# Moving the value products inside a round, and a first-group norm built from four columns

## The chip, the core and the metric

The kernel runs on one core of one Trainium2 chip. A core has a matrix engine (PE in the profile), a vector engine (DVE), a scalar engine for activations (ACT), a general engine (POOL) and a queue that issues transfers (SP). Each takes its own instructions strictly in the order of the program and waits on semaphores for the others. The metric is device microseconds (us) of one execution.

## The reference

Causal attention (4 batches, 12 heads, 448 positions, head size 64) is followed by an RMS norm and a gated feed-forward layer, all in float32:

```python
scores = where(mask, -1e9, q @ k.T / 8); attn = softmax(scores)
x = (attn @ v)                       # joined over heads: 1792 tokens x 768
rms = sqrt(mean(x * x, axis=-1) + 1e-6)
xn = x / rms * rms_g
g = xn @ w_gate
out = (g * sigmoid(g) * (xn @ w_val)) @ w_out
```

## The kernel before

The tokens are cut into three groups. The first is 512 tokens: the first 256 queries of two batches. It has 12 attention units (numbers 0 to 11 here; a unit is one pair of heads of one batch), and units 12 to 23 belong to the second group. The feed-forward products of one group are interleaved with the attention of the next. The order on every engine is written by hand: a list of steps is run one by one, each step is one tick, and `post(n, f)` runs `f` after n more ticks. The table `T` holds those delays, and `READY_X` holds the ticks from which each part of x may be used.

The first stage consists of rounds of six steps. Round p issues, in program order: the score products of unit p+3 (`scores`, L191), the products of the probabilities with v of unit p (`products`, L274) with the copy of their result into x (L289), the transposes of the first head of unit p+1 (L248, into bank t), two free steps, and the transposes of the second head of unit p+1 (L248, into bank x). Around this stand:

- the softmax on DVE: mask and minimum (L200), then the exponentials on ACT (L203) and the sum with a tiny bias (L226), then reciprocals on DVE (`rs`, L212), then scaling by them on POOL (L208, four instructions a unit);
- copies of the transposes out of PSUM into `pt`: the first head on ACT (L254), the second on DVE (L252); the products with v need both;
- the unpacking of weights (`w_c` L374 on ACT, `w` L375 on POOL, L377 and L379 on DVE) and their split into a high and a low part (`w_h` L389 on ACT, `w_l` L391 on DVE or L102 on POOL), and the same split of x (`xh` L325 on ACT, `xl` L326 on DVE);
- the early parts of the feed-forward product (`ffn_part`, L435 to L437, three matmuls each), which stand in the two free steps.

The norm: `square` squares each finished 128 x 512 part of x on POOL and adds it to `acc` on POOL. After the sixth part, `rms` multiplies `acc` by a matrix of ones (L333, result 128 x 512, the same in every row), ACT takes the root (L335), and DVE takes the reciprocal in four pieces (L338). The first use of it is `gr` (L449), on DVE, which empties the first accumulator of the feed-forward product; `t_sb` (a tanh on ACT, L450, then L451 on DVE) follows. Bank t has one buffer, so that a new user of it waits until the reader of the last one is done.

Of the kernel before, what the change touches and what calls it, by code (L numbers as in the profile page):

```python
# [10 lines left out]
F32 = mybir.dt.float32  # L11
# [3 lines left out]
ALU = mybir.AluOpType  # L15
AF = mybir.ActivationFunctionType
# [4 lines left out]
DM = H * D  # L21
DFF = 1536
P = 128
NP = H // 2
# [3 lines left out]
W = 512  # L28
# [10 lines left out]
        for g in range(NG) for c in range(NP)}  # L39
ENDS = [max(i for i, u in enumerate(UNITS) if u[0] == g) + 1 for g in range(NG)]  # L40
# [1 line left out]


T = dict(c0=0, c1=1, c2=4, c20=9, c3=5, c30=10, c5=7, c50=14, exp=1, exp0=3, gt=1, hh=1, hl=4, ws=5, ld2=7,
         ld=4, ld1=11, lv=5, norm0=7, norm1=2, r1=5, so=3, wl=2, wl0=8, xl=2, xl0=9)
LOAD = (4, 12, 24, 36, 48, 60, 74)
CONVERT = (20, 32, 44, 62, 76)
SPLIT = (33, 45, 57)

READY_W, READY_X = (45, 57, 68), (40, 52, 64, 76, 87)  # L50
WR = 4
WARM = [9, 0, 0, 2]
EXTRA = 4
# [8 lines left out]
def attention_ffn(ctx: ExitStack, tc: tile.TileContext, qk0, qk1, qk2, v, v2, w, g, out, out2):  # L62
# [7 lines left out]
    nc = tc.nc  # L70
# [3 lines left out]
    def pool(name, bufs, at=ctx, **kw):  # L74
        return at.enter_context(tc.tile_pool(name=name, bufs=bufs, **kw))
# [3 lines left out]
    ps = pool("ps", 1, space=PSUM)  # L79
    wr_p = pool("wr", WR, side="left")  # L80
    ws_p = pool("ws", 4, side="left")
    ht_p = pool("ht", 4, ffn, side="left")
    rm_p = pool("rm", 1, ffn, side="left")
# [7 lines left out]
    st_p = pool("st", 5, att, side="right")  # L91

    def bank(tag, bufs=1):


        return ps.tile([P, W], F32, tag=tag, name=tag + "_ps", bufs=bufs)
# [4 lines left out]
    def pool_op(out_, a, op, b):  # L101
        nc.gpsimd.tensor_tensor(out_, a, b, op=op)  # L102


    ident = const.tile([P, P], F32, name="ident")
# [12 lines left out]
    ones = const.tile([P, P], F32, name="ones")  # L118
    nc.vector.memset(ones, 1.0)
    eps = const.tile([P, 1], F32, name="eps")  # L120
# [9 lines left out]
    def post(delay, fn):  # L130
        if delay <= 0:
            fn()
        else:
            later.setdefault(now[0] + delay, []).append(fn)
# [7 lines left out]
    xr, xh, xl, acc, xq = {}, {}, {}, {}, {}  # L142
# [15 lines left out]
    def load_v(p):  # L158
        if p < len(UNITS):
            _, kind, _, _, row, _ = UNITS[p]  # L160
            raw_v[p] = raw.tile([P, 2, 4, 2, D], F32, tag="v", name="v_r", bufs=3)
            if kind == 2:
                nc.sync.dma_start(out=raw_v[p][: KB[2]], in_=v2[row])
            else:
                nc.sync.dma_start(out=raw_v[p][:, 0, : NKB[kind]], in_=v[row, :, : NKB[kind]])
# [67 lines left out]
    def steps_t(p):  # L233

        if not 0 <= p < len(UNITS):
            return []
        _, kind, _, _, _, _ = UNITS[p]
        pr = hs[p]
        kb = KB[kind]

        def some(e):
            pt = pr["pt", e] = pt_p.tile([P, W], F32, tag=f"pt{e}", name="pt")
            ps = bank("x" if e and p < ENDS[1] + 1 else "t")
            at = 0
            for j in range(NKB[kind]):
                for o, wd in blocks(kind):
                    if kb * j < wd:
                        nc.tensor.transpose(ps[:kb, at: at + P],  # L248
                                            pr["sp"][e][:, o + kb * j: o + kb * (j + 1)], ident)
                        at += P  # L250
            if kind or (e and p < ENDS[0]):
                nc.vector.tensor_copy(pt[:kb, :at], ps[:kb, :at])  # L252
            else:
                nc.scalar.copy(pt[:kb, :at], ps[:kb, :at])  # L254

        return [lambda e=e: some(e) for e in (0, 1)]

    def steps_a(p):


        if not 0 <= p < len(UNITS):
            return []
        g_, kind, c, k, _, base = UNITS[p]
        pr = hs[p]
        kb, nq = KB[kind], QUERIES[kind]

        def products():
            for h in range(1 + (kind == 2)):
                at = 0
                for j in range(NKB[kind]):  # L270
                    q0, n = ((0, 2 * P), (P, P))[j] if kind == 0 else (D * h, (P, D)[kind - 1])
                    a0 = at + (D * h if kind == 2 else 0)
                    for e in (0, 1):
                        nc.tensor.matmul(  # L274
                            av_ps[e * D: (e + 1) * D, p % 2, q0: q0 + n], raw_v[p][:kb, h, j, e, :],
                            pr["pt", e][:kb, a0: a0 + n], start=(j == 0), stop=(j == NKB[kind] - 1))
                    at += n if kind == 0 else P

        def copy():
            if g_ == 2 and base == 0:  # L280
                if c < 3:
                    xq[c] = w64_p.tile([P, 2, XT], F32, tag="w64", name="xq")
                xr[g_, c] = xq[c % 3][:, c // 3]
            elif base == 0:
                xr[g_, c] = xr_p.tile([P, W], F32, tag="xr", name="xr")
            x = xr[g_, c][:, base: base + nq]
            if p == LAST[g_, c]:
                post(2, lambda: square(g_, c))
            (nc.scalar.copy if g_ == 1 else nc.vector.tensor_copy)(x, av_ps[:, p % 2, :nq])  # L289

        return [products, copy]


    rinv, waiting, ff = {}, [], {}

    def square(b, c):

        halves = [(0, HX), (HX, XT)] if b == 2 else [(0, W)]
        for j, (lo, hi) in enumerate(halves):
            x = xr[b, c][:, lo: hi]  # L300
            sq = rm_p.tile([P, W], F32, tag="sq", name="sq") if c else \
                rm_p.tile([P, W], F32, tag="acc", name="acc", bufs=2)
            sq = sq[:, : hi - lo]
            if b:
                nc.scalar.activation(sq, x, AF.Square)
            else:
                pool_op(sq, x, ALU.mult, x)
            if c == 0:
                acc[b, j] = sq
            else:  # L310
                pool_op(acc[b, j], acc[b, j], ALU.add, sq)
        if b == 2:
            return
        if c == NP - 1:
            post(T["r1"], lambda: rms(b, acc[b, 0]))
        waiting.append((b, c))

    def split_x():
# [8 lines left out]
            out=l, in0=x, scalar=gc, in1=f32(h), op0=ALU.mult, op1=ALU.subtract))  # L327
        xh[b, c], xl[b, c] = h, l

    def rms(b, sq):  # L330

        ps = bank("t")
        nc.tensor.matmul(ps, ones, sq, start=True, stop=True)  # L333
        r = rinv[b] = rm_p.tile([P, W], F32, tag="rms", name="rms", bufs=2)
        nc.scalar.activation(r, ps, AF.Sqrt, bias=eps, scale=1.0 / DM)  # L335
        for i in range(W // P):
            sl = slice(i * P, (i + 1) * P)
            post(i if b else 0, lambda sl=sl: nc.vector.reciprocal(r[:, sl], r[:, sl]))  # L338


    w64 = w.bitcast(I32).rearrange("u p (c t) -> u p c t", t=2)
# [388 lines left out]
    def round_steps(p):  # L730

        noop = [lambda: None]
        (s_, ts) = (f or noop for f in (steps_s(p + DP), steps_t(p + 1)))
        as_ = steps_a(p)

        def products():
            for f in as_:
                f()


        def scores():
            if p + 2 > 0:
                post(T["lv"], lambda: load_v(p + 2))
            s_[0]()

        def both():
            scores()
            products()

        ts = (ts + noop)[:2]  # L750
        return [both] + ts if p > ENDS[0] else [scores, products, ts[0]] + 2 * noop + ts[1:]

    def round_of_two(p):

# [28 lines left out]
    with tc.manual_schedule():  # L783
# [9 lines left out]
        for p in range(-DP, ENDS[1]):  # L793
            steps += round_steps(p)
            if p + 1 in ENDS:
                ends.append(len(steps))
# [10 lines left out]
        def at_tick(n, fn):  # L807
            prep.setdefault(n, []).append(fn)
# [7 lines left out]
        n = 0  # L816
        for t_, s, c in early:
            n = max(n, t_)
            while n % 6 not in (3, 4) and n < 87:
                n += 1  # L820
            at_tick(n, lambda s=s, c=c: ffn_part(s, (c,)))
            n += 1
# [19 lines left out]
        for s in range(2 * NU):  # L842
# [9 lines left out]
            n = s + 6 - 2 * NU  # L852
# [5 lines left out]
            for k0 in (0, 2, 4):  # L858
# [3 lines left out]
                i = 3 * (s % NU) + k0 // 2 + 1  # L862
# [14 lines left out]
                n = 3 * (s - 2 * NU + 2) + k0 // 2  # L877
# [26 lines left out]
        for v in range(NF):  # L904
            if v % 3 == 1 and v < 9:
                wo_sums(v // 3)
            for i in range(7):
                ps_ = quad_product(v, i)
                quad_result(v, i, ps_)
                if v + 1 < NF:  # L910
                    n = (0, 1, None, 2, None, 3, None)[i]
# [7 lines left out]
                if v + 2 < NF:  # L919
                    n = (None, None, 0, 1, None, 2, 3)[i]  # L920
# [18 lines left out]
        for q in range(21):  # L939
            i, p = divmod(q, 3)  # L940
# [58 lines left out]
```

## Time and profile before

| | |
|---|---|
| median of 3 runs | 700.14 us (699.67 to 701.06) |
| profiled execution | 702.16 us |
| its span, first to last instruction | 700.4 us |
| PE, DVE, ACT, POOL busy in 20 to 40 us | 15.89, 18.39, 16.30, 19.87 of 20 |
| the same in 40 to 60 us | 16.83, 13.22, 14.30, 16.88 of 20 |
| the same in 60 to 80 us | 15.79, 14.43, 15.49, 12.21 of 20 |
| the same in 80 to 100 us | 17.93, 19.89, 16.47, 9.44 of 20 |
| the same in 100 to 120 us | 20.00, 19.07, 13.60, 12.28 of 20 |

How to read it: the span begins at 0, the first stage goes to about 74 us, and then the feed-forward part of the first group starts, with the second group's attention between. Matmuls overlap, so a busy share of PE says little by itself; the waits say more. The granted clock of PE is 0.99 on average; stretches below 1.0 stand in the table by stretches.

### The profile page before, as it was taken

Reading aid. Unit: us, or ns where it says so; the run is one execution under the profiler, and the core shown is the slowest. Engines: PE = TensorE matmul, PEld = TensorE weight load, DVE = VectorE, ACT = ScalarE, POOL = GpSimd, SP = SyncE. Lnnn points to the kernel's source line nnn. Section 1 sums busy time; section 2 is a strip of 40 time slices with the busy share of each in tenths; the row PEclk is TensorE's granted clock in tenths of the full one; section 3 lists DMA queues with packets and bytes.
Section 4 is the critical chain, followed back from the end, with each engine's and each line's share of the span. In section 5 each row is a group of like instructions: output and inputs, shape, how many; then the busy total and the mean of one; then the engine's idle time right before and its main releaser. Section 6 shows DMA issues by size and latency. Waiting matters only on the chain. (4 is left out here: it accounts for less than half of the span.)

```text
span 700.4 us, 11930 instructions
## 1 busy us (share of the span) xinstructions
PE 671.0 (96%) x4106; PEld 550.9 (79%) x4106; DVE 536.9 (77%) x1029; ACT 371.6 (53%) x832; POOL 361.9 (52%) x313
## 2 busy tenths in 40 slices
PE   9878889999999999999999999997999999999997
PEld 6445667777777768777777777886999999999987
DVE  4976899989997667777687877396386868679973
ACT  6967876777685435436445353451433342445540
POOL 4988445545548534665776565552363536302220
PEclk9999999999999999999999999998999999999999
DMA  8746486868778547576767655333567576562541
GB/s 267 259 146 205 146 281 222 281 232 277 233 280 302 193 117 263 164 258 194 251 190 237 212 155 177 118 120 109 162 204 250 177 246 223 168 165 86 171 119 67
DMA packets 71355, 138.80 MB, mean 198 GB/s; under 512 B 7744, under 2 KB 39232, under 8 KB 71296
## 3 DMA queue, kind: packets, MB, share of 16 engines
q1 hardware_dynamic: 71296, 138.05, 60.3%
q8 instruction: 32, 0.52, 0.3%
q14 instruction: 27, 0.22, 0.1%
HBM read 104.21 MB, written 33.82 MB: 197 GB/s over the span
## 5 line engine op out<-in xcount | busy, mean ns | idle before, releaser
L208 POOL TENSOR_SCALAR sp<-sp,rs 128x384 f32<-128x384 f32 (+3 forms) x132 | 89.5, 696 | 95.8 <-DVE rs L212 84.8
L435 PE MATMUL m_ps<-xh,w_h 128*128 128x512 f32 x282 | 120.2, 426 | 3.7 <-DVE rs L212 3.7
L203 ACT ACTIVATE sp<-sp,nm 128x384 f32<-128x384 f32 (+3 forms) x168 | 87.2, 522 | 47.7 <-DVE nm L200 47.1
L437 PE MATMUL m_ps<-xh,w_l 128*128 128x512 f32 x282 | 111.3, 395 | 0.0
L436 PE MATMUL m_ps<-xl,w_h 128*128 128x512 f32 x282 | 111.1, 394 | 0.0
L102 POOL TENSOR_TENSOR a_l<-w_q,a_h 128x768 fp32r<-128x768 f32 x24 | 47.4, 1977 | 75.7 <-ACT a_h L473 75.6
L375 POOL TENSOR_SCALAR w<-w 128x768 f32<-128x768 f32 x36 | 46.5, 1292 | 53.1 <-ACT w_c L374 47.0
L274 PEld LDWEIGHTS a_ps<-pt,v_r 128*64 128x64 f32 (+1 forms) x864 | 40.7, 137 | 36.2 <-issue 11.1
L274 PE MATMUL a_ps<-pt,v_r 128*64 128x128 f32 (+2 forms) x864 | 57.1, 268 | 9.7 <-DVE pt L252 7.3
L435 PEld LDWEIGHTS m_ps<-xh,w_h 128*128 128x128 f32 x282 | 53.3, 189 | 16.1 <-issue 8.0
L437 PEld LDWEIGHTS m_ps<-xh,w_l 128*128 128x128 f32 x282 | 53.4, 189 | 12.1
L252 DVE COPY pt<-t_ps 128x384 f32<-128x384 f32 (+1 forms) x71 | 42.5, 598 | 26.6 <-PE t_ps L248 26.4
L437 PE MATMUL m_ps<-hh,w_l 128*128 128x512 f32 x144 | 57.8, 401 | 4.3 <-DVE w_l L391 3.9
L102 POOL TENSOR_TENSOR w_l<-w_r,w_h 128x768 fp32r<-128x768 f32 x30 | 59.2, 1979 | 3.6 <-ACT w_h L389 3.4
L436 PEld LDWEIGHTS m_ps<-xl,w_h 128*128 128x128 f32 x282 | 53.6, 190 | 7.8
L435 PE MATMUL m_ps<-hh,w_h 128*128 128x512 f32 x144 | 59.2, 411 | 0.0
L200 DVE CUSTOM_DVE_ANT_0 sp<-s_ps,mask 128x128 f32<-128x128 f32 (+3 forms) x136 | 49.8, 415 | 11.1 <-PE s_ps L191 9.3
L436 PE MATMUL m_ps<-hl,w_h 128*128 128x512 f32 x144 | 57.1, 397 | 0.0
L248 PE MATMUL t_ps<-ident,sp 128*128 128x128 f32 (+1 forms) x309 | 50.9, 277 | 1.4 <-ACT rms L335 0.8
L377 DVE SCALAR_TENSOR_TENSOR w<-w 128x768 int32<-128x768 int32 x36 | 45.4, 1261 | 8.0 <-POOL w L375 8.0
L248 PEld LDWEIGHTS t_ps<-ident,sp 128*128 128x128 f32 (+1 forms) x309 | 38.1, 138 | 16.7 <-POOL sp L208 2.6
L473 ACT CAST a_h<-w_q 128x768 fp32r<-128x768 f32 (+1 forms) x48 | 35.0, 753 | 24.9 <-PE m_ps L436 19.1
(176 smaller groups left out, 1702.1 us busy)
## 6 DMA issues: line engine op xcount, KB each, us to landing
w<-in_w SPq DMA_DIRECT2D x36, 768.0 KB, 5.9
w<-w_c SPq DMA_DIRECT2D x36, 384.0 KB, 2.7
w_r<-w SPq DMA_DIRECT2D x36, 384.0 KB, 4.5
qk_r<-in_qk SPq DMA_DIRECT2D x48, 256.0 KB, 4.0
qk_r<-in_qk SPq DMA_DIRECT2D x12, 512.0 KB, 5.6
v_r<-in_v SPq DMA_DIRECT2D x12, 448.0 KB, 5.1
v_r<-in_v SPq DMA_DIRECT2D x24, 192.0 KB, 3.4
wy<-w_r SPq DMA_DIRECT2D x24, 192.0 KB, 4.9
```

Of the source, the lines that this page charges most:

```text
L102: nc.gpsimd.tensor_tensor(out_, a, b, op=op)
L200: nc.vector.tensor_tensor_reduce(out=sp, in0=ps, in1=mk, scale=nsc, scalar=3.0e38, op0=ALU.add, op1=ALU.min, accum_out=nm)
L203: post(T["exp" if p >= ENDS[0] else "exp0"], lambda: nc.scalar.activation(sp, sp, AF.Exp, bias=nm, scale=-1.0, accum_out=sm))
L208: pr["norms"].append(lambda: nc.gpsimd.tensor_scalar(sp, sp, rs, 1.0, op0=ALU.mult, op1=ALU.mult))
L248: nc.tensor.transpose(ps[:kb, at: at + P], pr["sp"][e][:, o + kb * j: o + kb * (j + 1)], ident)
L252: nc.vector.tensor_copy(pt[:kb, :at], ps[:kb, :at])
L274: nc.tensor.matmul(av_ps[e * D: (e + 1) * D, p % 2, q0: q0 + n], raw_v[p][:kb, h, j, e, :], pr["pt", e][:kb, a0: a0 + n], start=(j == 0), ...
L375: (T["c1"], lambda: nc.gpsimd.tensor_scalar(hf_, hf_, 0.0, 1.0, op0=ALU.mult, op1=ALU.mult)),
L377: (T["c2" if s >= 5 else "c20"], lambda: nc.vector.scalar_tensor_tensor(out=lo, in0=lo, scalar=29, in1=hi, op0=ALU.logical_shift_right, op ...
L435: nc.tensor.matmul(ps, wh[:, k, :], mh, start=(first and k == ks[0]), stop=False)
L436: nc.tensor.matmul(ps, wh[:, k, :], ml, start=False, stop=False)
L437: nc.tensor.matmul(ps, wl[:, k, :], mh, start=False, stop=(last and k == 5))
```

## The change

In rounds before round 11 the first transposes now come right after the scores, one step earlier, and the products with v come in the fourth step instead of the second. The early parts of the feed-forward product move to steps three and five. Rounds 11 and 12 keep the old order.

For the first group the norm is computed in another way. The last square is made on DVE and is not added to `acc`. Eight matmuls with a single column of ones give the sums of squares of 128 tokens each as one column (`acc` and the last square accumulate in PSUM), so that the root and the reciprocal are taken of a 128 x 4 tile. The four columns are written on the diagonals of a 128 x 512 tile (two on ACT, two on DVE), and a product with ones spreads them over all rows; ACT copies the result out. The delay from the last square to this norm is 2 ticks (`r0`); the old one (`r1`) is 5.

```diff
-READY_W, READY_X = (45, 57, 68), (40, 52, 64, 76, 87)
+READY_W, READY_X = (45, 57, 68), (42, 54, 66, 78, 89)
...
+            elif c == NP - 1:
+                nc.vector.tensor_tensor(sq, x, x, op=ALU.mult)
...
-            else:
+            elif b or c < NP - 1:
                 pool_op(acc[b, j], acc[b, j], ALU.add, sq)
...
+        if c == NP - 1 and b == 0:
+            post(T["r0"], lambda: rms_first(acc[0, 0], sq))
...
+    def rms_first(a, sq):
...
+        ps = bank("t")[:, :n]
+        for i in range(n):
+            sl = slice(P * i, P * (i + 1))
+            nc.tensor.matmul(ps[:, i: i + 1], a[:, sl], ones[:, :1], start=True, stop=False)
+            nc.tensor.matmul(ps[:, i: i + 1], sq[:, sl], ones[:, :1], start=False, stop=True)
+        nc.scalar.activation(rc, ps, AF.Sqrt, bias=eps, scale=1.0 / DM)
+        def diagonal():
+            nc.vector.reciprocal(rc, rc)
+            for i in range(n):
+                d = dg[:, P * i: P * (i + 1)]
+                if i % 2:
+                    nc.scalar.mul(d, ident, rc[:, i: i + 1])
+                else:
+                    nc.vector.tensor_scalar_mul(d, ident, rc[:, i: i + 1])
+        def spread():
+            ps = bank("t")
+            nc.tensor.matmul(ps, ones, dg, start=True, stop=True)
+            nc.scalar.copy(r, ps)
+        post(2, diagonal)
+        post(4, spread)
...
-        return [both] + ts if p > ENDS[0] else [scores, products, ts[0]] + 2 * noop + ts[1:]
+        if p > ENDS[0]:
+            return [both] + ts
+        if p in (ENDS[0] - 1, ENDS[0]):
+            return [scores, products, ts[0]] + 2 * noop + ts[1:]
+        return [scores, ts[0]] + noop + [products] + noop + ts[1:]
...
-            while n % 6 not in (3, 4) and n < 87:
+            while n % 6 not in (2, 4) and n < 87:
```

PE, one round in the middle of the first stage. L191 are the scores, L274 the products with v, L248 into t_ps and x_ps the two transposes. Before:

```order
L191 MATMUL s_ps<-qk_r 128x128 x2
L191 MATMUL s_ps<-qk_r 128x256 x2
L274 MATMUL a_ps<-pt,v_r 64x256 x2
L274 MATMUL a_ps<-pt,v_r 64x128 x2
L248 MATMUL t_ps<-ident,sp 128x128 x3
L435 MATMUL m_ps<-xh,w_h 128x512
L436 MATMUL m_ps<-xl,w_h 128x512
L437 MATMUL m_ps<-xh,w_l 128x512
L248 MATMUL x_ps<-ident,sp 128x128 x3
```

Now (L469 to L471 are what L435 to L437 were):

```order
L191 MATMUL s_ps<-qk_r 128x128 x2
L191 MATMUL s_ps<-qk_r 128x256 x2
L248 MATMUL t_ps<-ident,sp 128x128 x3
L469 MATMUL m_ps<-xh,w_h 128x512
L470 MATMUL m_ps<-xl,w_h 128x512
L471 MATMUL m_ps<-xh,w_l 128x512
L274 MATMUL a_ps<-pt,v_r 64x256 x2
L274 MATMUL a_ps<-pt,v_r 64x128 x2
L248 MATMUL x_ps<-ident,sp 128x128 x3
```

The transposes into t and a feed-forward part now stand between the scores and the products.

ACT, the end of the first stage, from the copy of unit 12's first transposes on. Before (L203 are the exponentials of unit 15, L335 root and table of the norm, L450 the first tanh):

```order
L254 COPY pt<-t_ps 128x384
L325 ACTIVATE xh<-xr,g_sb 128x512
L254 COPY pt<-x_ps 128x384
L203 ACTIVATE sp,sm<-sp,nm 128x128
...
L289 COPY xr<-a_ps 128x256
L335 ACT_TABLE_LOAD
L335 ACTIVATE rms<-t_ps,eps 128x512
L254 COPY pt<-t_ps 128x384
L374 ACTIVATE w_c<-w_728 128x768
L389 CAST w_h<-w_c 128x768
L450 ACT_TABLE_LOAD
L450 ACTIVATE t_sb<-gr 128x512
```

Now (L345 is the root of the four columns, L352 the diagonal, L359 the copy of the spread norm):

```order
L345 ACT_TABLE_LOAD
L345 ACTIVATE rc<-t_ps,eps 128x4
L254 COPY pt<-x_ps 128x384
L352 ACTIVATE dg<-ident,rc 128x128 x2
L203 ACT_TABLE_LOAD
L203 ACTIVATE sp,sm<-sp,nm 128x128
...
L289 COPY xr<-a_ps 128x256
L254 COPY pt<-t_ps 128x384
L359 COPY rms<-t_ps 128x512
L408 ACTIVATE w_c<-w_724 128x768
L423 CAST w_h<-w_c 128x768
L484 ACTIVATE t_sb<-gr 128x512
```

The root now stands ahead of unit 15's exponentials, a load of the exponentials' table has come between them, the load ahead of the tanh is gone, and the copy of unit 13's transposes out of bank t stands behind the exponentials and ahead of the copy of the norm.

PE at the same place, now, from the first columns on (L358 is the spreading product). Unit 15's scores stand behind the columns:

```order
L343 MATMUL t_ps<-ones,acc 128x1
L344 MATMUL t_ps<-ones,sq 128x1
...
L248 MATMUL x_ps<-ident,sp 128x128 x3
...
L191 MATMUL s_ps<-qk_r 128x128 x2
L191 MATMUL s_ps<-qk_r 128x256 x2
...
L274 MATMUL a_ps<-pt,v_r 64x256 x2
...
L248 MATMUL t_ps<-ident,sp 128x128 x3
L358 MATMUL t_ps<-dg,ones 128x512
```

Before, L333 stood behind those scores and products, directly ahead of the last transposes shown. On DVE, the last square stands behind the unpacking steps L377 and L379 and the fifth `xl`, and ahead of the sixth `xl` and unit 15's softmax; in every odd round `xl` has moved from ahead of the softmax to behind the reciprocals `rs`. On POOL, one unpacking step (L375) has moved ahead of a square and its sum in round 8, and the last square with its sum is gone.

## Rows read from the trace of the kernel before

**Rows 1.** Waits by pair, 0 to 66.7 us: total us, times, longest.

```profile
POOL sp L208 <- DVE rs L212: 12.9, 6, 7.2
...
PE a_ps L274 <- DVE pt L252: 6.7, 5, 1.8
```

**Rows 2.** Timeline 34 to 46 us: start, duration, engine, line, [idle before <- releaser].

```profile
37.26 0.86 PE L274 MATMUL a_ps<-pt,v_r 128*64 128x256 f32 x6 [1.82 <-DVE pt L252]
...
38.64 0.48 ACT L254 COPY pt<-t_ps 128x384 f32<-128x384 f32 x1 [2.44 <-PE t_ps L248]
...
41.12 0.81 ACT L389 CAST w_h<-w_c 128x768 fp32r<-128x768 f32 x1
...
41.96 0.96 DVE L391 TENSOR_TENSOR w_l<-w_c,w_h 128x768 fp32r<-128x768 f32 x1 [2.21 <-ACT w_h L389]
...
45.18 0.17 DVE L212 RECIPROCAL rs<-sm 128x4 f32<-128x4 f32 x1
```

**Rows 3.** Timeline of POOL alone, two places.

```profile
25.08 3.81 POOL L208 TENSOR_SCALAR sp<-sp,rs 128x128 f32<-128x128 f32 x4
...
45.55 1.64 POOL L208 TENSOR_SCALAR sp<-sp,rs 128x128 f32<-128x128 f32 x4 [1.93 <-DVE rs L212]
```

**Rows 4.** Timeline 59 to 79 us, the end of the first stage.

```profile
59.52 0.93 PE L191 MATMUL s_ps<-qk_r 64*128 64x128 f32 x8
...
61.13 0.28 DVE L200 CUSTOM_DVE_ANT_0 sp<-s_ps,mask 128x128 f32<-128x128 f32 x1
...
62.98 0.49 PE L248 MATMUL x_ps<-ident,sp 128*128 128x128 f32 x3
...
64.10 0.93 PE L191 MATMUL s_ps<-qk_r 64*128 64x128 f32 x8
...
65.53 0.28 DVE L200 CUSTOM_DVE_ANT_0 sp<-s_ps,mask 128x128 f32<-128x128 f32 x1
...
65.85 0.40 ACT L203 ACTIVATE sp<-sp,nm 128x128 f32<-128x128 f32 x1 [0.84 <-DVE nm L200]
...
66.64 0.17 DVE L212 RECIPROCAL rs<-sm 128x4 f32<-128x4 f32 x1
...
67.95 0.35 ACT L289 COPY xr<-a_ps 128x256 f32<-128x256 f32 x1
68.32 1.28 ACT L335 ACT_TABLE_LOAD   x1
...
68.71 1.12 PE L333 MATMUL t_ps<-acc,ones 128*128 128x512 f32 x2 [1.98 <-POOL acc L102]
69.87 0.69 ACT L335 ACTIVATE rms<-t_ps,eps 128x512 f32<-128x512 f32 x1 [0.27 <-PE t_ps L333]
70.59 3.39 DVE L338 RECIPROCAL rms<-rms 128x128 f32<-128x128 f32 x4 [3.78 <-ACT rms L335]
...
73.58 1.28 ACT L450 ACT_TABLE_LOAD   x1
...
74.08 0.69 DVE L449 TENSOR_TENSOR gr<-m_ps,rms 128x512 f32<-128x512 f32 x1
...
74.87 0.63 ACT L450 ACTIVATE t_sb<-gr 128x512 f32<-128x512 f32 x1
...
75.53 0.69 DVE L451 SCALAR_TENSOR_TENSOR t_sb<-t_sb,gr 128x512 f32<-128x512 f32 x1 [0.68 <-ACT t_sb L450]
```

**Rows 5.** Timeline at 441 us: the third group's norm, which has this form already.

```profile
441.08 1.39 PE L493 MATMUL t_ps<-ones,acc 128*128 128x1 f32 x12
...
443.03 0.99 ACT L502 ACTIVATE dg<-ident,rc 128x128 f32<-128x128 f32 x3 [0.26 <-DVE rc L496]
```

**Rows 6.** Table by stretches: PE, PEld, DVE, ACT, POOL busy (instructions), PE clock, DMA, GB/s.

```profile
72.00:74.00 2.00, 2.00 (x7) 1.59 (x7) 1.98 (x3) 1.98 (x4) 1.07 (x2) 0.52 0.00 0
...
92.00:94.00 2.00, 2.00 (x11) 1.23 (x12) 1.99 (x4) 1.94 (x6) 1.32 (x1) 0.50 0.99 387
```

**Rows 7.** Timeline at 90 us, PE.

```profile
90.04 0.47 PE L435 MATMUL m_ps<-xh,w_h 128*128 128x512 f32 x1 [2.07 <-DVE rs L212]
```

More of the change, by code (lines that the diff above doesn't have):

```diff
@@ L44 @@
 T = dict(c0=0, c1=1, c2=4, c20=9, c3=5, c30=10, c5=7, c50=14, exp=1, exp0=3, gt=1, hh=1, hl=4, ws=5, ld2=7,
-         ld=4, ld1=11, lv=5, norm0=7, norm1=2, r1=5, so=3, wl=2, wl0=8, xl=2, xl0=9)
+         ld=4, ld1=11, lv=5, norm0=7, norm1=2, r0=2, r1=5, so=3, wl=2, wl0=8, xl=2, xl0=9)
 LOAD = (4, 12, 24, 36, 48, 60, 74)
@@ L313, in square @@
             return
-        if c == NP - 1:
+        if c == NP - 1 and b == 0:
+            post(T["r0"], lambda: rms_first(acc[0, 0], sq))
+        elif c == NP - 1:
             post(T["r1"], lambda: rms(b, acc[b, 0]))
@@ L328, in split_x @@
         xh[b, c], xl[b, c] = h, l
+    def rms_first(a, sq):
+        n = W // P
+        rc = st_p.tile([P, n], F32, name="rc", bufs=1)
+        dg = ht_p.tile([P, W], F32, tag="t", name="dg")
+        r = rinv[0] = rm_p.tile([P, W], F32, tag="rms", name="rms", bufs=2)
+        ps = bank("t")[:, :n]
[18 more added lines that the diff above has]
+        post(4, spread)
     def rms(b, sq):
@@ L337, in rms @@
             sl = slice(i * P, (i + 1) * P)
-            post(i if b else 0, lambda sl=sl: nc.vector.reciprocal(r[:, sl], r[:, sl]))
+            post(i, lambda sl=sl: nc.vector.reciprocal(r[:, sl], r[:, sl]))
     w64 = w.bitcast(I32).rearrange("u p (c t) -> u p c t", t=2)
```

## The prediction

> **What bounds the kernel now.** I read the table by stretches first, then the waits of the first stage, then the timeline at its two ends. The first stage, to about 74 us, is bound by no engine alone. PE waits 6.7 us in five places for the second half of the probabilities that DVE copies [rows 1], and POOL, which scales the probabilities, waits 12.9 us in six places for DVE's reciprocals, 7.2 of them before its first work [rows 1]; so at most 12.9 - 7.2 = 5.7 us of POOL's time in this stage were free. The two waits hang together. At 37.26 PE had stood 1.82 us at the products with v; the transposes behind them came late, so ACT's copy of these waited 2.44, so its split of a weight ended at 41.93, so DVE stood 2.21 before `w_l`, and the reciprocals at 45.18 were late for POOL [rows 2], which had idled 1.93 [rows 3].
>
> The end of the stage is one chain. Scores of unit 14 start at 59.52; PE waits 1.98 for POOL's sum; product, root and DVE's four reciprocals (3.39) follow, and `gr` starts at 74.08, 14.56 us after those scores [rows 4]. DVE stood 3.78 before the reciprocals [rows 4]. Afterwards DVE is the full engine: it is busy 1.99 of 2.00 us at 92 to 94 [rows 6], and PE waited 2.07 at 90.04 for an accumulator that DVE empties late [rows 7]. So what counts is when `gr` starts: every microsecond by which it comes later goes on through DVE's queue.
>
> **Moving the products (term A).** No instruction is added. PE's 6.7 us of waits go, because four steps instead of two lie between the second transposes and the products. But what is next in PE's queue is a transpose that needs POOL's scaled probabilities, so PE gains only what POOL can give. The bounds are 0 and POOL's 5.7 us. I follow the one chain above: without PE's stall ACT, `w_h` and the reciprocals come early enough and POOL's 1.93 goes; its other waits follow a weight that POOL itself unpacks, and PE does not feed those. The moved `xl` (0.7 to 1 us out of the way of a softmax, and behind it into the way of the copy) and the moved unpacking step I count as nothing. I take -2.0, the end near the row of that wait; scores of unit 14 start about 2 us earlier.
>
> A row speaks for little gain: four scalings on POOL take 1.64 us at 45.55 and 3.81 at 25.08 [rows 3], with nothing but DVE's unpacking different around them. The Trainium skill ("SBUF — State Buffer", section "SBUF: two separate sides") says why: DVE and GpSimd share a port pair under an exclusive lock, and whoever comes second blocks fully. By that rule idle time freed on POOL is partly refilled by DVE's held port; by the idle time alone A could be -5.7.
>
> **The norm of the first group (term B).** I lay the new order out from the start of unit 14's scores, with durations of the old trace.
>
> - DVE: in the old trace the softmax of unit 14 started at 61.13 and the softmax of unit 15 at 65.53, 4.40 us with unpacking, copies and one `xl` between [rows 4]. Another `xl` stood ahead of the first and is now behind. So the softmax starts when the scores end (0.93 + 0.1), and the same run ends at about 5.2 (less the 0.2 that DVE waited there). Then comes the new square; DVE had none, and the nearest row of two 512-wide operands is `gr`, 0.69 [rows 4]. It ends at 5.9.
> - PE is done with its other work at about 3.5 (scores, products, transposes, two feed-forward parts) and stands 2.4 us at the columns, in place of the 1.98 at the sum. The columns: 1.39 us for 12 [rows 5], 1.7 for the 15 behind the square: 7.6.
> - Behind them on PE, which they now hold up: second transposes, a feed-forward part, scores of unit 15, from 62.98 to the end of the scores at 65.03 [rows 4], 2.05: 9.65.
> - DVE's softmax of unit 15 and `rs`, 65.53 to 66.64 [rows 4] and 0.1 to start: 10.85; the reciprocal of 128 x 4, like `rs` 0.17: 11.1. ACT's half of the diagonal waits for it: three took 0.99 [rows 5], two take 0.7: 11.85 (DVE's half lies beside it).
> - ACT now loads the exponentials' table behind the diagonal, 1.28 [rows 4]: 13.15. Exponentials, sum and the copy of x follow, 65.85 to 68.30 [rows 4]: 15.6. The copy out of bank t, 0.48 [rows 2]: 16.1. Only then is bank t free for the spreading product, so PE stands there from about 12.2.
> - Spreading product like L333, 1.12, and ACT's copy, between 0.5 and the root's 0.69 [rows 4]: `gr` at 17.8, against 14.56. That is +3.2.
>
> Both earlier waits of about 2 us (1.98 and 2.07) were followed by a stretch at half clock: granted 0.52 at 72 to 74 and 0.50 at 92 to 94 [rows 6]. A wait of 2.4 at the columns will do so too, and the stretch then falls on the 2.05 us of PE work behind them. Bounds: 0 and +2.1; half of the stretch met the chain in the old case, so I take +0.8. B = +4.0, bounds +3.2 and +5.3.
>
> **Behind `gr` (term C).** The old trace had ACT's weight steps done while DVE took reciprocals; the tanh started 0.79 after `gr`, and DVE waited 0.68 for it [rows 4]. Now two weight steps (0.8 each, `w_h` in [rows 2]) stand between the copy of the norm and the tanh: it starts about 1.6 after `gr`. C = +0.8, bounds 0 and +0.9. The table load that went from ahead of the tanh (73.58 to 74.86) was hidden then [rows 4] and gives nothing back. The 3.39 of reciprocals are inside the 14.56 and counted by B. POOL loses a square and a sum; nothing waits for POOL at that place any more.
>
> A page makes the table dearer. The Trainium skill ("ScalarE: Activation LUTs", section "What ACT_TABLE_LOAD costs") gives 1283 ns plus a drain of about 1380 ns. In the trace the tanh started at 74.87, right behind the load [rows 4], so no drain is seen; by the page B would be 1.4 more.
>
> **Sum.** -2.0 + 4.0 + 0.8 = +2.8 us, on the profiled execution 702.16 + 2.8 = 705.0. That execution lies 2.0 above the median, so the median should go from 700.14 to 702.9. Ends of the terms: -5.7 + 3.2 = -2.5, less 1.0 for the half-clock stretch at 92 to 94 if it goes (half of 2 us [rows 6]), -3.5; and 0 + 5.3 + 0.9 = +6.2.
>
> **Rivals.**
>
> 1. Faster: the first stage runs ahead. If PE's waits really held everything, POOL gives up all its 5.7 us, unit 14's scores start 5.7 earlier, and no half clock meets the chain: -5.7 + 3.2 + 0 = -2.5, 697.6. For it: PE's waits add up to more than A. Against it: POOL's durations grow when DVE is beside it [rows 3]. It decides from A beyond -4.0. Chance 0.22.
> 2. No change: DVE's lateness is taken up behind `gr`. PE then reaches 90 us later, its stall of 2.07 and the half clock behind it go (2.07 + 1.0 [rows 6, 7]), and these 3.1 pay the 2.8: 699.8. Against it: DVE, not PE, was full there. Chance 0.20.
> 3. Much slower: A gives nothing because PE now waits for POOL at the transposes, and half clock meets all 2.05 us: 0 + 5.3 + 0.8 = +6.1, 706.2; from half of that on, beyond 704.9. The drain of the page would also end here. Chance 0.13.
>
> My forecast, 701.5 to 704.9, has 0.45.
>
> **Numbers.** About 0.2%, 1.4 us, is what a measurement can tell here. Slower: 0.45 + 0.13 = 0.58; same 0.20; faster 0.22. The time is 702.9. The range of eight in ten leaves some of rival 1 and of rival 3 out: 698.0 to 705.4.
>
> **What would show it.** In the changed profile: no wait of PE for `pt` in the first 55 us, but waits at the first transposes for POOL; unit 14's scores near 57.5; PE idle over 2 us at the columns and over 3 us at the spreading product, the latter put down to ACT's copy of `pt`; a table load between diagonal and exponentials; `gr` at about 75.5 to 76.5. I am wrong if `gr` starts before 74, or if it starts later and the stretch at 90 us does not move with it.

## The result and the profile after

The changed kernel takes 708.35 us in the median of 4 executions (707.71 to 709.95), against 700.08 for the kernel before: ratio 1.012, 95% interval 1.0099 to 1.014. It is 8.3 us slower, where 2.8 were predicted, and outside the range. The profiled execution took 709.95 us, its span is 708.2, and its mean granted clock of PE is 0.981, against 0.990 in the profile before.

First the waits in the first 66.7 us of the changed kernel (columns as in [rows 1]):

```profile
PE t_ps L248 <- POOL sp L208: 4.9, 5, 2.4
PE t_ps L344 <- DVE sq L307: 1.4, 1, 1.4
...
PE a_ps L274 <- DVE pt L252: 0.3, 1, 0.3
...
POOL sp L208 <- DVE rs L212: 12.0, 6, 7.6
```

The 6.7 us at the products with v are down to 0.3, and 4.9 us at the transposes stand in their place: POOL's own waits shrank only from 12.9 to 12.0. That is term A with little behind it.

Then the end of the first stage in the changed kernel, by the timeline (start, duration, engine, line, form, idle before and its releaser); it answers to [rows 4]:

```profile
58.42 0.93 PE L191 MATMUL s_ps<-qk_r 64*128 64x128 f32 x8
...
63.43 0.68 DVE L307 TENSOR_TENSOR sq<-xr 128x512 f32<-128x512 f32 x1
...
64.17 0.38 PE L344 MATMUL t_ps<-ones,sq 128*128 128x1 f32 x2 [1.35 <-DVE sq L307]
...
65.11 0.57 PE L343 MATMUL t_ps<-ones,acc 128*128 128x1 f32 x2
...
65.54 0.56 PE L344 MATMUL t_ps<-ones,sq 128*128 128x1 f32 x2
...
66.82 0.88 PE L248 MATMUL x_ps<-ident,sp 128*128 128x128 f32 x3
...
68.91 1.65 PE L191 MATMUL s_ps<-qk_r 64*128 64x128 f32 x8
...
70.70 0.29 DVE L200 CUSTOM_DVE_ANT_0 sp<-s_ps,mask 128x128 f32<-128x128 f32 x1 [5.79 <-PE s_ps L191]
...
72.09 0.69 ACT L352 ACTIVATE dg<-ident,rc 128x128 f32<-128x128 f32 x2 [3.88 <-DVE rc L348]
...
72.79 1.28 ACT L203 ACT_TABLE_LOAD   x1
...
76.43 0.48 ACT L254 COPY pt<-t_ps 128x384 f32<-128x384 f32 x1
...
76.96 1.12 PE L358 MATMUL t_ps<-dg,ones 128*128 128x512 f32 x2 [3.08 <-ACT pt L254]
...
78.12 0.59 ACT L359 COPY rms<-t_ps 128x512 f32<-128x512 f32 x1 [1.22 <-PE t_ps L358]
...
78.51 0.63 PE L471 MATMUL m_ps<-xh,w_l 128*128 128x512 f32 x1
...
79.24 0.69 DVE L483 TENSOR_TENSOR gr<-m_ps,rms 128x512 f32<-128x512 f32 x1 [6.55 <-PE m_ps L471]
...
80.13 0.64 ACT L484 ACTIVATE t_sb<-gr 128x512 f32<-128x512 f32 x1
...
80.47 1.85 POOL L102 TENSOR_TENSOR w_l<-w_c,w_h 128x768 fp32r<-128x768 f32 x1
...
80.80 2.07 DVE L485 SCALAR_TENSOR_TENSOR t_sb<-t_sb,gr 128x512 f32<-128x512 f32 x1 [0.78 <-ACT t_sb L484]
```

Every station of the prediction is there and in its order: square, wait at the columns, diagonal, table, copy of bank t, spread. The durations are not. From 64.68 on the column products start 0.43 us apart, and the scores take 1.65 instead of 0.93. The row of `gr` says what released it: not ACT's copy (it ended at 78.71) but `m_ps`, the feed-forward product that stands behind the spread in PE's queue. PE's clock in these stretches (columns: stretch, its length, PE busy, granted clock, DMA share, GB/s):

```profile
64.00:66.00 2.00, 1.83 (x11) 0.65 0.33 129
66.00:68.00 2.00, 2.00 (x10) 0.50 0.00 0
68.00:70.00 2.00, 2.00 (x11) 0.50 0.00 0
70.00:72.00 2.00, 2.00 (x9) 0.65 0.20 24
78.00:80.00 2.00, 2.00 (x8) 0.56 0.00 0
96.00:98.00 2.00, 1.68 (x4) 0.50 0.86 262
98.00:100.00 2.00, 2.00 (x9) 0.50 0.89 343
100.00:102.00 2.00, 2.00 (x12) 0.50 0.78 229
```

0.50 is the lower level, 1.2 GHz. The stall of [rows 7] is there too, later and longer, with that half clock behind it:

```profile
96.32 0.77 PE L469 MATMUL m_ps<-xh,w_h 128*128 128x512 f32 x1 [3.09 <-DVE rs L212]
```

The loss isn't all in this stage. I took the same instruction in both timelines and subtracted its starts:

| instruction | before | after | difference |
|---|---|---|---|
| unit 14's scores | 59.52 | 58.42 | -1.10 |
| first `gr` | 74.08 | 79.24 | +5.16 |
| third `gr` | 92.48 | 98.76 | +6.28 |
| fifth `gr` | 113.36 | 120.76 | +7.40 |
| ninth `gr` | 155.09 | 160.58 | +5.49 |
| 23rd `gr` | 411.21 | 416.35 | +5.14 |
| ACT's first copy of `m` | 497.50 | 505.17 | +7.67 |
| span | 700.4 | 708.2 | +7.8 |

Two steps surprise. From the fifth to the ninth `gr`, 1.9 us come back: the profiled execution of before had a stall of PE of 1.38 at 152.64 that this one hasn't (the profiled execution of before was 2.0 above its median). And 2.5 us are lost around 500 us, where the change edits nothing. The rows there, of the kernel before and then of the changed one:

```profile
497.50 0.48 ACT L601 COPY m<-m_ps 128x384 f32<-128x384 f32 x1 [1.30 <-PE m_ps L578]
```

```profile
502.22 0.43 SPq L479 DMA_DIRECT2D out_t<-ob  x1
...
505.17 0.48 ACT L635 COPY m<-m_ps 128x384 f32<-128x384 f32 x1 [4.21 <-DMA out_t<-ob]
...
505.70 0.45 PE L612 MATMUL m_ps<-ch,a_h 128*128 128x384 f32 x1 [1.92 <-ACT m L635]
```

Before, ACT's copy waited for PE; now it waits for a DMA that carries the last output tile `ob` out, and PE waits for the copy. `gr`, `t_sb` and `ob` take turns in a ring of four buffers (`ht_p`, tag `t`; each new tile takes the next buffer of the four): 24 + 24 + 12 = 60 turns in the whole program, so the last `ob` sits in the fourth buffer. The diagonal `dg` takes a turn of the same ring, 61 in all, and the last `ob` sits in the first. When the ring is closed the next stage's tiles lie on its memory. My theory became: the copy's target `m1` lies on that first buffer.

### The profile page after: what moved, and what is told of

It reads as the page before. It is cut to its first block, busy times and chain, and to the rows that moved or that the text cites. A ratio compares the mean times of both kernels' runs of the same rounds, so it can differ in the third digit from the quotient of the medians.

```text
span 708.2 us, 11956 instructions
## 1 busy us (share of the span) xinstructions
PE 679.1 (96%) x4122; PEld 555.7 (78%) x4122; DVE 537.0 (76%) x1029; ACT 372.4 (53%) x835; POOL 360.4 (51%) x311
## 5 line engine op out<-in xcount | busy, mean ns | idle before, releaser
L469 PE MATMUL m_ps<-xh,w_h 128*128 128x512 f32 x282 | 121.8, 432 | 3.1 <-DVE rs L212 3.1
L471 PE MATMUL m_ps<-xh,w_l 128*128 128x512 f32 x282 | 112.3, 398 | 0.0
L203 ACT ACTIVATE sp<-sp,nm 128x384 f32<-128x384 f32 (+3 forms) x168 | 87.2, 522 | 47.1 <-DVE nm L200 44.6
L469 PEld LDWEIGHTS m_ps<-xh,w_h 128*128 128x128 f32 x282 | 53.8, 191 | 16.8 <-issue 8.7
L471 PEld LDWEIGHTS m_ps<-xh,w_l 128*128 128x128 f32 x282 | 53.8, 191 | 12.2
L471 PE MATMUL m_ps<-hh,w_l 128*128 128x512 f32 x144 | 57.5, 399 | 4.3 <-DVE w_l L425 3.9
L274 PEld LDWEIGHTS a_ps<-pt,v_r 128*64 128x64 f32 (+1 forms) x864 | 40.3, 138 | 24.8 <-issue 10.8
L469 PE MATMUL m_ps<-hh,w_h 128*128 128x512 f32 x144 | 59.1, 411 | 0.0
L248 PE MATMUL t_ps<-ident,sp 128*128 128x128 f32 (+1 forms) x309 | 51.7, 277 | 5.6 <-POOL sp L208 4.9
L248 PEld LDWEIGHTS t_ps<-ident,sp 128*128 128x128 f32 (+1 forms) x309 | 38.1, 138 | 23.2 <-POOL sp L208 11.8
L274 PE MATMUL a_ps<-pt,v_r 128*64 128x128 f32 (+2 forms) x864 | 55.2, 271 | 0.7 <-DVE pt L252 0.7
L411 DVE SCALAR_TENSOR_TENSOR w<-w 128x768 int32<-128x768 int32 x36 | 46.9, 1302 | 5.5 <-POOL w L409 5.5
L413 DVE SCALAR_TENSOR_TENSOR w_c<-w_c,w 128x768 int32<-128x768 int32 x36 | 48.0, 1332 | 0.6
```

Of the source, the lines that this page charges most:

```text
L203: post(T["exp" if p >= ENDS[0] else "exp0"], lambda: nc.scalar.activation(sp, sp, AF.Exp, bias=nm, scale=-1.0, accum_out=sm))
L248: nc.tensor.transpose(ps[:kb, at: at + P], pr["sp"][e][:, o + kb * j: o + kb * (j + 1)], ident)
L274: nc.tensor.matmul(av_ps[e * D: (e + 1) * D, p % 2, q0: q0 + n], raw_v[p][:kb, h, j, e, :], pr["pt", e][:kb, a0: a0 + n], start=(j == 0), ...
L411: (T["c2" if s >= 5 else "c20"], lambda: nc.vector.scalar_tensor_tensor(out=lo, in0=lo, scalar=29, in1=hi, op0=ALU.logical_shift_right, op ...
L413: (T["c3" if s >= 5 else "c30"], lambda: nc.vector.scalar_tensor_tensor(out=ti, in0=ti, scalar=3, in1=lo, op0=ALU.logical_shift_left, op1= ...
L469: nc.tensor.matmul(ps, wh[:, k, :], mh, start=(first and k == ks[0]), stop=False)
```

## The experiments

Theory: the norm carries the loss, in three faults (columns ahead of unit 15's scores with half clock, the spread behind ACT's copy, and the ring). Rivals: the shift of the products costs by itself; the loss needs both parts. Ratios are to the kernel before, run beside each experiment on the same chip; there its single executions scatter from 697.2 to 703.5 us, and one took 705.6. The changed kernel itself was measured only in the first series (1.012), so that a difference between its ratio and that of an experiment compares two chips; where their intervals overlap, the difference in time is not shown.

**The two parts apart.** `e1_products_only` takes the norm back:

```diff
-        if c == NP - 1 and b == 0:
-            post(T["r0"], lambda: rms_first(acc[0, 0], sq))
-        elif c == NP - 1:
+        if c == NP - 1:
             post(T["r1"], lambda: rms(b, acc[b, 0]))
```

(and the last square to POOL); `e2_norm_only` does the reverse, the new norm in the old order.

> The changed order of the first stage alone (products with v two slots later, the first ffn parts at the new slots), with the first group's norm as it was before. Theory (the norm carries the whole loss): unit 14's scores start near 58.4 us as in the changed kernel, against 59.5 before; the norm behind them takes 14.6 us as before; the time is 699.0 us, 1.1 below before (698.2 to 700.2). Rival (the shift costs by itself: POOL's normalisation is waited for by the first transposes, 2.4 us at 37, and half the clock follows): 702 us or more, that is a third or more of the 8.3 us.

> The order of before with the new norm of the first group alone (DVE's square, columns, diagonal, spread). Theory (the norm carries the whole loss): first gr near 80 us instead of 74.1, half clock at the columns, behind the spread and behind the stall that then falls near 97; 708 to 710 us. Rival (the loss needs both parts, the shift of the products being what leaves PE short of work): 700 to 704 us.

The shift alone: 699.84 us against 700.80, ratio 0.9994 (0.9976 to 1.0012). The norm alone: 709.30, ratio 1.0134 (1.0106 to 1.0162). So the norm carries the whole loss, and the shift is worth nothing that can be measured (the interval leaves room for the 1.1 us that were expected, not for the rival's loss), although in its profile too the transposes wait 4.9 us for POOL, and from 36 to 42 us PE's granted clock is 0.72 on average. Both rivals fall.

**The ring.** `e6_dg_elsewhere` gives `dg` the squares' buffer; `e7_extra_tile` adds one turn to the kernel before and nothing else.

```diff
-        dg = ht_p.tile([P, W], F32, tag="t", name="dg")
+        dg = rm_p.tile([P, W], F32, tag="sq", name="dg")
```

```diff
+    extra = ht_p.tile([P, W], F32, tag="t", name="extra")
+    nc.vector.memset(extra[:, :1], 0.0)
```

> The changed kernel with the diagonal in the buffer of the squares (sq) instead of a turn in the ring of four buffers from which gr, t_sb and the output tiles ob come. Theory (the extra turn moves the last ob onto the buffer that the next stage's first result m1 reuses, so that ACT's copy of m waits 4.2 us for the DMA of ob, at 505 us): that copy waits for PE again, 1.3 us, and the time falls by about 2.6 us to 705.7; the first 480 us stay as they are. Rival (the wait is company of a PE that is late anyway, or comes from another new tile): the wait for the DMA stays, or goes without the time falling; 708 to 708.5 us.

> The kernel before, with one more turn in the ring of four buffers at the program's start (a tile of which DVE sets one column and which nobody reads), and nothing else. Theory (the turn alone costs in the last stage): the first 480 us as before, then ACT's copy of m waits about 4 us for the DMA of the last ob; 2.6 us over before, 702.7 to 703.5 us. Rival (the turn costs nothing by itself): 700.5 us, within 0.3 per cent of before.

ACT's copy in the timeline of e6 (with DVE's first `u` behind it), then of e7:

```profile
501.84 0.48 ACT L635 COPY m<-m_ps 128x384 f32<-128x384 f32 x1 [1.29 <-PE m_ps L612]
...
504.80 0.56 DVE L640 TENSOR_TENSOR u<-m,s_ps 128x384 f32<-128x384 f32 x1 [3.39 <-DMA out_t<-ob]
```

```profile
498.99 0.48 ACT L603 COPY m<-m_ps 128x384 f32<-128x384 f32 x1 [4.24 <-DMA out_t<-ob]
```

The wait goes with the turn and comes with it. In the profiles of all seven kernels that have the 61st turn (changed, e2, e3, e4, e5, e7, e10) it is 4.15 to 4.24 us for the DMA, in all seven that have 60 (before, e1, e6, e8, e9, e11, e12) 1.29 or 1.30 for PE. With 60 turns the DMA is still waited for, but later: in e6 it releases DVE's first `u`, 3.0 us behind ACT's copy. So the turn decides which of the next stage's tiles gets the late buffer, as the theory has it; where the tiles lie in memory was not read out. e7 takes 703.57 us against 701.35, ratio 1.0034 (1.002 to 1.0048): one unread tile costs 2.2 us, nearly 500 us after it was made. e6 takes 707.71, ratio 1.0092 (1.0069 to 1.0116), 2.0 us less by the ratios than the changed kernel's 1.012, but these two intervals overlap. So the wait is shown from both sides, and its price in time by e7.

**The columns.** `e4_columns_later` sets `r0=4` (behind unit 15's scores), `e10_columns_between` `r0=3` (behind the third feed-forward part, ahead of the scores), both in the changed kernel's `r0=2`.

> The changed kernel with the column products issued two steps later, behind unit 15's scores, instead of ahead of them; the diagonal and the spread move with them. Theory (the columns hold up unit 15's scores by PE's wait for DVE's square and by running at half clock: 6.3 us from the wait's start to the scores): scores of unit 15 near 65 us instead of 68.9, no half clock from 64.5 to 71, first gr near 76 although the root comes later; 703 to 706 us. Rival (the root is the path, so that a later root is a later gr): gr at 80 or later, 709 us or more. Second rival (half clock in that stretch comes from the columns themselves, wherever they stand): half clock again behind them, and 706 to 708 us.

> The changed kernel with the column products one step later: behind the second transposes and the third ffn part, still ahead of unit 15's scores. DVE's square is done by then, so PE does not wait ahead of the columns. Theory (the half clock came with PE's wait at the columns, not with the columns): clock 1.00 from 62 to 72, softmax of unit 15 starts 7.6 us behind that of unit 14 (5.8 in e4_columns_later and eight columns of 0.22 us), against 11 in the changed kernel; gr near 75 to 76; 704.5 to 706.5 us. Rival (eight one-column products bring the half clock wherever they stand ahead of the scores): clock near 0.6 behind the columns, softmax of unit 15 over 9 us behind unit 14's, gr at 77 or later, 706.5 to 708.5 us.

e4 takes 705.79 us, ratio 1.0068 (1.0041 to 1.0094); e10 703.22, ratio 1.0043 (1.0022 to 1.0064). Unit 15's scores in e4, the spread and `gr`; then PE's clock in e10 (columns as above), its first column, the spread and `gr`:

```profile
62.84 0.93 PE L191 MATMUL s_ps<-qk_r 64*128 64x128 f32 x8
...
71.42 1.12 PE L358 MATMUL t_ps<-dg,ones 128*128 128x512 f32 x2 [3.06 <-ACT dg L352]
...
73.92 0.69 DVE L483 TENSOR_TENSOR gr<-m_ps,rms 128x512 f32<-128x512 f32 x1 [6.56 <-PE m_ps L471]
```

```profile
66.00:68.00 2.00, 2.00 (x14) 0.68 0.00 0
68.00:70.00 2.00, 2.00 (x7) 0.50 0.22 81
...
64.78 0.28 PE L343 MATMUL t_ps<-ones,acc 128*128 128x1 f32 x2
...
72.49 1.12 PE L358 MATMUL t_ps<-dg,ones 128*128 128x512 f32 x2 [0.57 <-ACT pt L254]
...
74.42 0.69 DVE L483 TENSOR_TENSOR gr<-m_ps,rms 128x512 f32<-128x512 f32 x1 [4.21 <-PE m_ps L471]
```

From unit 14's scores to unit 15's it is 10.49 us in the changed kernel, 5.81 in e4 and 7.50 in e10. So the place of the columns is worth some 3.6 to 5.4 us of time by the ratios (1.012 - 1.0068, 1.012 - 1.0043); neither interval reaches that of the changed kernel. e10 came out under both of its ranges. On the clock my theory for it fell: PE does not wait at the columns there, and half clock comes behind them all the same; it only meets less of the chain. I can't say what brings it: in e4 the same eight products stand behind the scores and 64 to 72 us run at 1.00. In e4 `gr` starts where it did before (73.92 against 74.08), and the time is still above before's by 0.68%, of which the ring is half. In its profile about 3 us more go around a wait of PE for DVE at 515.83 (2.21, then a granted clock of 0.57 to 520); in the changed kernel's this wait is 0.6 us. Why it grew there I leave open.

**The waits filled.** `e5_filled` puts products that nobody reads into PE's two waits:

```diff
+        for _ in range(2):
+            nc.tensor.matmul(full[:, W // 2:], ones, a[:, W // 2:], start=True, stop=True)
...
+            for _ in range(5):
+                nc.tensor.matmul(fill[:, W // 2:], ones, acc[0, 0][:, W // 2:], start=True, stop=True)
```

> The changed kernel with products that nobody reads put into PE's two waits: two of 256 columns ahead of the column products (into the unused part of their bank) and five ahead of the spread. Theory (half clock after these two waits delays the chain: columns, scores of unit 15 and the ffn part behind the spread): clock 1.00 from 64 to 72 and from 77 to 82, scores of unit 15 near 67.3 us instead of 68.9, first gr near 77 instead of 79.2, 704.5 to 706.5 us. Rival (half clock comes from the column products themselves, or the chain runs through ACT and DVE alone): clock near 0.6 again from 64 to 72, gr within 0.5 us of 79.2, 708 us or more.

```profile
66.00:68.00 2.00, 2.00 (x12) 0.72 0.00 0
68.00:70.00 2.00, 2.00 (x10) 0.50 0.00 0
...
78.00:80.00 2.00, 2.00 (x16) 1.00 0.00 0
```

Behind the spread the clock holds, behind the columns it doesn't. `gr` starts at 78.25, 1.0 earlier, but the time is 710.8 us (705.83 to 711.14), ratio 1.012 (1.0092 to 1.0148): no gain. That the half clock is worth its microseconds of path is read from durations below; this run does not show it in the time, and no other run isolates it.

**The spread.** `e3_spread_bank` lets it use a bank of the scores:

```diff
-            ps = bank("t")
+            ps = bank("s", 2)
             nc.tensor.matmul(ps, ones, dg, start=True, stop=True)
```

> The changed kernel with the spreading product in a bank of the scores instead of the transposes' bank t, so that it does not wait for ACT's copy of pt. Theory (PE stands 3.1 us for that copy, and the next ffn part with gr's second input stands behind it): spread near 74 instead of 77.0, ACT's copy of it right behind pt at 76.9, first gr near 77.6 instead of 79.2, no half clock at 77.5 to 82; 705 to 706.7 us. Rival (the path goes through ACT's exponentials and copies, so PE's wait is only company): gr within 0.3 us of 79.2 and 708 us.

```profile
76.90 0.60 ACT L359 COPY rms<-s_ps 128x512 f32<-128x512 f32 x1
77.53 0.69 DVE L483 TENSOR_TENSOR gr<-m_ps,rms 128x512 f32<-128x512 f32 x1 [4.75 <-ACT rms L359]
```

`gr` at 77.53 as expected, now released by ACT's copy; the spread runs at 73.89 without a wait. The time is 706.48 us, ratio 1.0084 (1.0056 to 1.0113), within the theory's range and 2.5 us under the changed kernel by the ratios, though the intervals overlap. On the path the theory holds: the single buffer of bank t costs PE's 3.1 us of standing, and `gr` comes 1.7 us earlier without it.

**Mended.** `e12_columns_ring` joins e4 and e6. `e8_all` adds the scores' bank and moves the whole diagonal and the copy to DVE. `e9_tanh_first` also sets one weight cast behind the first tanh, and `e11_old_order` is e9 in the order of before.

```diff
-                if i % 2:
-                    nc.scalar.mul(d, ident, rc[:, i: i + 1])
...
-            nc.scalar.copy(r, ps)
+            nc.vector.tensor_copy(r, ps)
...
-                if k0 == (0 if s < 3 else 4):
+                if k0 == (0 if 0 < s < 3 else 4):
```

(the last edit is e9's).

> The changed kernel with two of the mends only: columns behind unit 15's scores and the diagonal in the buffer of the squares; the spread still in bank t behind ACT's copy, ACT still makes half of the diagonal. Theory (the two faults add: columns' place 3.6 us by e4_columns_later, the ring 2.0 to 2.4 us by e6_dg_elsewhere and e7_extra_tile): ratio to before 1.003 to 1.005, that is 702.5 to 704 us, and no wait of ACT for the DMA of ob. Rival (e4_columns_later lost its time in the last stage for another reason than the ring): 1.006 or more, 705 us.

> The changed kernel with its four faults mended: columns behind unit 15's scores, the diagonal in the buffer of the squares and wholly on DVE, the spread in a bank of the scores, its copy on DVE. Theory (norm and ring carry the whole loss and the new form is worth its work when nothing queues behind it): gr near 70.5 us against 74.1 before, no wait for the DMA of ob, no half clock at 64 to 82; 695 to 699 us. Rival (what gr gains is lost in the stall for the accumulator near 90 or in the waits for converted weights behind it): 699.5 to 701.5 us.

> The mended kernel (e8_all) with one edit more: the first weight cast of the steady stage (ACT's w_h of the fourth weight tile) two steps later, so that it stands behind the first tanh and POOL's split of it is later too. Theory (gr's gain of 2.5 us in e8_all was lost because tanh stood behind that cast and DVE's next product beside POOL's split took 2.0 us instead of 0.7): tanh starts at 73 or before, DVE's product behind it takes 0.7 us near 73.7, PE's stall near 90 ends 1.5 to 2 us earlier, at 88; 697 us on this scale (1.5 to 2 under e8_all). Rival (the cast is waited for soon after, so the loss comes back as a wait for converted weights): the stall stays at 89.8 us, 698.5 to 700 us.

> The mended norm with the late cast (e9_tanh_first) on the order of before, so that the only difference from e9_tanh_first is where the products with v and the first ffn parts stand. Theory (the shift of the products is worth little, about 1 us, since POOL's normalisation takes the place of DVE's copy as what PE waits for): 698 to 700.5 us, within 0.2 per cent of e9_tanh_first. Rival (the shift is what makes the mended version level with before): 702 us or more. Second rival (the shift costs, through half clock at 37 us in most executions): 696 to 698 us.

| | median us, then that of before | ratio | first, third `gr` |
|---|---|---|---|
| e12 | 702.33, 700.55 | 1.0017 (0.9995 to 1.0039) | 76.44, 94.80 |
| e8 | 698.98, 701.35 | 0.9984 (0.9964 to 1.0004) | 71.56, 92.29 |
| e9 | 699.48, 700.53 | 0.9984 (0.9961 to 1.0006) | 70.32, 90.92 |
| e11 | 699.30, 700.55 | 0.9996 (0.9977 to 1.0015) | 71.36, 91.80 |

The two faults add up: e12 came out a little below the ratio of 1.003 to 1.005 that was expected, and ACT's copy waits 1.30 for PE there. e8 and e9 undo the whole loss and lie over 1% below the changed kernel; against before both intervals reach past 1, so a gain over it isn't shown. e11 agrees with e9 within 0.2%, so the shift of the products stays worth nothing measurable.

In e8 `gr` starts 2.5 us earlier than before and the third `gr` only 0.2: the rival's mechanism held (PE stalls 3.01 us ahead of 89.84 there), although 698.98 us still lies at the upper end of the theory's range. The rows of e8, then of e9:

```profile
72.99 0.85 ACT L419 CAST w_h<-w_c 128x768 fp32r<-128x768 f32 x1
...
73.72 0.66 ACT L480 ACTIVATE t_sb<-gr 128x512 f32<-128x512 f32 x1
...
74.06 1.80 POOL L102 TENSOR_TENSOR w_l<-w_c,w_h 128x768 fp32r<-128x768 f32 x1
...
74.41 2.01 DVE L481 SCALAR_TENSOR_TENSOR t_sb<-t_sb,gr 128x512 f32<-128x512 f32 x1 [2.07 <-ACT t_sb L480]
```

```profile
72.39 0.98 DVE L481 SCALAR_TENSOR_TENSOR t_sb<-t_sb,gr 128x512 f32<-128x512 f32 x1 [1.30 <-ACT t_sb L480]
73.30 2.57 DVE L407 SCALAR_TENSOR_TENSOR w<-w 128x768 int32<-128x768 int32 x1
```

e9 frees the tanh, DVE's product takes 0.98 instead of 2.01, and the next unpacking step takes 2.57 (0.95 at 76.34 in e8) beside POOL's split, which now starts at 73.16. From the first to the third `gr` it is 20.7 us in e8 and 20.6 in e9: the slow stretch moved to the next instruction, and the theory for e9 fell. PE's stall does end at 88.48, 1.4 us earlier than in e8, but unit 14's scores, which stand ahead of the edit, had started 1.2 earlier already (57.29 against 58.53).

## Why the prediction was wrong

The direction, the stations and their order were right, and so were their releasers but for that of `gr`. The sum was 5.0 us short on the profiled execution (705.0 predicted, 709.95 measured) and 5.4 by the medians. By its own steps:

- **Term A**, -2.0: -1.1. The row against it, POOL's 3.81, was the one to follow: PE's waits moved to POOL, and unit 14's scores start at 58.42, not near 57.5. Executions differ here: in the ten profiles with the new order these scores start at 57.03 to 59.15, in the four with the old one at 59.21 to 60.91, so that some lead is there; by e1 nothing measurable of it reaches the time. 0.9 us of the miss.
- **Term B**, +4.0: +6.3 (14.56 to 79.24 - 58.42 = 20.82). Without the clock the laid-out path was right to 0.2 us: the square ended at 5.7 (5.9 predicted), and PE stood 1.35 for it at the columns (2.4 predicted). Its step to 11.1 leaves out the 0.17 of `rs` itself, which starts at 66.64; the measured stretch from that softmax to the end of the reciprocal, 1.36, came out at the 1.35 that was laid out. The step that failed is "half of the stretch met the chain in the old case, so I take +0.8". All of it met the chain, behind the columns and again behind the spread: columns 2.65 us instead of 1.7, transposes and feed-forward part 2.09 instead of 1.12, scores to softmax 1.79 instead of 1.03, and behind the spread the feed-forward product into `m_ps` let `gr` start 0.53 after the end of ACT's copy. That is 0.95 + 0.97 + 0.76 + 0.53 = 3.2 against 0.8. My upper bound of +2.1 counted only the 2.05 us of work behind the columns; the columns themselves, and `gr`'s second input behind the spread, were not in it. The 3.2 are read from this profile alone: in e6, with the same order, unit 15's scores came 9.20 us behind unit 14's instead of 10.49, the spreading product took 1.62 instead of 1.12, and `gr` came 20.34 behind unit 14's scores instead of 20.82.
- **Term C**, +0.8: +1.1 to the third `gr`, for another reason. Tanh started 0.89 after `gr`, not 1.6, since `gr` waited for PE while ACT did its weight steps. But DVE's product behind it took 2.07 beside POOL's split, against 0.69 in [rows 4]. The Trainium skill ("SBUF — State Buffer", section "SBUF: two separate sides") has DVE and GpSimd share a port pair under an exclusive lock, and the one that comes second blocks. The traces agree: in the seven kernels where this product started early in POOL's split it ended 0.54 to 0.56 us behind the end of the split, and in e9, where it missed the split, the next DVE instruction was the long one. I had used that rule for A and not here. 0.3 us of the miss.
- **Term D**, the half-clock stretch at 92 to 94, taken as 0: it moved with the stall, as I said it would, and grew with it (2.07 to 3.09 of wait, half clock from 96 to 102). +1.1 to the fifth `gr`.
- **The missing term.** I counted the diagonal's instructions, not its buffer. The ring costs 2.2 us by e7 (2.0 by the ratio of e6, with overlapping intervals), and 2.5 in the profile. No wait of the first stage could show it; the turns had to be counted.
- In the profiled pair, 2.3 us came back between the fifth and the 23rd `gr`. The prediction had no term for that. So 0.9 + 2.3 + 0.3 + 1.1 + 2.5 - 2.3 = 4.8 of the 5.0.

Rival 3 (A gives nothing because PE waits for POOL at the transposes, full half clock, 706.2) was nearest, in its mechanism too; it lacked the ring. Rival 2 needed the stall at 90 to go; it moved, because `gr` moved with DVE's queue.

## What to carry to other kernels

Count a new tile's turn in its ring as a cost of its own: where a later stage reuses the ring's memory, the turn decides which of the last users it must wait for. Where a change makes PE wait ahead of work that others wait for, put that whole run of work at half clock into the upper bound, the new products included, and not half of it; and don't count on the wait as the only sign, since in e10 the half clock came without one. And a product put into PE's queue delays all that stands behind it; ask which input of the next step is queued there, besides the one that the product makes.

## What the runs showed of the hardware

- Eight one-column float32 products of 128 x 128 start 0.22 us apart at full clock (e4) and 0.43 at half (changed).
- The same order does not always meet the same clock: from 64 to 72 us the changed kernel ran at 0.57, e6, which has that order too, at 0.79, and the scores of unit 15 came 10.49 and 9.20 us behind those of unit 14. A price of half clock that is read from one profile holds for that execution.
- The 128 x 512 product of DVE behind the first tanh took 0.69 us where POOL's split of a weight was over or nearly so (before, e1, e4, e7, e12), and 1.96 to 2.07 where it started 0.30 to 0.41 us into the split (changed, e2, e3, e5, e6, e8, e10). In each of these seven it ended 0.54 to 0.56 us behind the split: what it lost was the rest of POOL's instruction.
